# Attention visits, output blocks and loads regrouped around the second and third tile of a linear-attention plus SwiGLU kernel

## Chip, cores, metric

One core of a Trainium2 chip. The metric is device time in microseconds (us) of one execution; lower is better. Before: 229.62 us, median of three runs (228.28 to 232.09).

## The reference, cut

Four sequences of 768 tokens with 8 heads of 64 go through a block-decayed linear attention with blocks of 64 tokens. Its output is `x` (3072 x 512), which goes through a SwiGLU feed-forward network (512 to 1536 to 512).

```python
for b in range(nb):                                  # 12 blocks of 64 tokens
    intra = (q_b @ k_b.T) * Dmask[None]              # decay mask inside the block
    intra = intra @ v_b
    inter = (q_b * lam_pow[None]) @ kv_state         # what earlier blocks left
    out[:, :, sl] = intra + inter
    kv_state = lam_block * kv_state + (k_b * rev_pow).T @ v_b
...
g = x @ w_gate
return (g * sigmoid(g)) * (x @ w_val) @ w_out
```

## The kernel before

The work is cut into 12 **groups**, each two blocks of 128 tokens of one sequence; two groups make a **tile** of 512 tokens, and there are six tiles. For each group the kernel loads k, q and v (512 KB each), casts k and scales q, transposes both (with a DMA from group 3 on, on PE before), and then visits the TensorE (PE) with small attention matmuls. For each tile it runs 12 feed-forward **steps** of eight matmuls of 512 columns (1.73 us; a half step has 256 columns and takes 0.87 us), and then four **output blocks** of 12 matmuls (2.59 us each), each followed by a write of 256 KB.

Attention work is hung between the steps by hand. The order in which it is written is the order on each engine, and PE does it all in that order. (The other engines stand under the profile's names: DVE is VectorE, ACT is ScalarE, POOL is GpSimd, SP is SyncE, which here only issues DMAs; PEld is PE's loading of weights.) While PE does feed-forward work for one tile, the attention of the next tile's groups is slipped in between.

```python
def load_group(g, parts="kqv"):
    for src, what in ((k, "kraw"), (q, "qraw"), (v, "v")):
        if what[0] in parts:
            load_fp32(g, nc.sync, src, what)      # the SP queue

def dma_transpose(g):
    t = st[("qk", g)]
    tt = qkt_pool.tile([128, 2, 2, HP, 128], BF16, name="qkt", tag="qkt")
    nc.sync.dma_start(out=..., in_=..., transpose=True)   # the SP queue too
    st[("qkt", g)] = tt

def cast_scaled(g, eng=nc.vector):
    t = qk_pool.tile([128, 2, 2, H * D], BF16, name="qk", tag="qk")
    st[("qk", g)] = t
    nc.scalar.copy(out=t[:, 0]..., in_=st[("kraw", g)]...)             # ACT casts k
    eng.tensor_tensor(out=t[:, 1]..., in0=st[("qraw", g)]..., in1=qfac(g), op=ALU.mult)  # DVE scales q
    dma_transpose(g)
# ...
def core_a(g):                    # inter: q against the state
    st[("op", g)] = [bank() for _ in range(2)]
    inter(g, True)
    guard(g)                      # a one-column ACT copy that orders inter before intra
def core_b(g, ...):               # intra: masked scores against v
    run_later(len(later))         # the masks (DVE)
    intra(g, False)
    evac(g, fns)                  # ACT copies the result to xt, the input of the tile's steps
def ahead(g):                     # what can be done before core
    upd(g)                        # state update of g: matmuls of k against scaled v
    scores(g)                     # k against q; needs the transpose of g
def attend(g):                    # core of g merged with ahead of g + 1
    run_later(len(later))
    core_a(g)
    if g + 1 < NG:
        upd_mm(g + 1); upd_copy(g + 1)
        scores(g + 1)
        late, later[:] = later[:], []
    core_b(g)
    if g + 1 < NG:
        later[:] = late
        state(g + 1)
# ... the plan: at(step, what) hangs `what` behind that step
s1a = [step(1, fc, 0, 2) for fc in range(FC)]     # second tile in half steps
s1b = [step(1, fc, 2, 4) for fc in range(FC)]
at(s1a[3], cast_scaled, 4)
at(s1a[3], load_group, 5)
for c in range(0, FC, 2):
    at(s1a[3], wo_piece, c, c + 2)                # output weights, 3 MB
# ...
at(s1b[3], cast_scaled, 5)
at(s1b[3], load_group, 6)
at(s1b[6], ahead, 4)
# ...
at(s1b[9], core_a, 4)
at(s1b[10], core_b, 4)
at(s1b[11], ffn_out, 0, 0)
at(s1b[11], ahead, 5)
at(s1b[11], run_later, 3)
at(s1b[11], ffn_out, 0, 1)
at(s1b[11], core_a, 5)
at(s1b[11], ffn_out, 0, 2)
at(s1b[11], core_b, 5)
at(s1b[11], cast_scaled, 6)
at(s1b[11], load_group, 7)
at(s1b[11], v_scale, 6, nc.gpsimd)
at(s1b[11], ffn_out, 0, 3)
outs = [(1, b) for b in range(4)]                 # second tile's outputs: inside the third
for t in range(2, NG // 2):
    ...                                           # steps, cast, load, attend, outputs
```

Loads and transposes leave from one engine's program, SP, in program order: a load written behind a transpose waits until the transposed data has been cast. And groups 0 to 5 load rows of 512 bytes and use a causal mask of double width; groups 6 to 11 load rows of 256 bytes. I call group 6's transpose T6, its loads k6, q6 and v6, and so on.

## Time and profile before

| quantity | before |
|---|---|
| median time | 229.62 us (229.02 with a fourth run) |
| PE busy | 218.5 of 227.1 us |
| largest PE wait after the start-up | 1.21 us |
| T6: issue to landing | 80.16 to 85.84 us |
| T6's data needed on PE | 88.1 us |

The page of the profile: the span, the busy times, and busy tenths in 40 slices of the span for PE and the DMA engines.

```profile
span 227.1 us, 5890 instructions
...
PE 218.5 (96%) x2432; PEld 118.2 (52%) x2444; DVE 90.1 (40%) x154; ACT 106.5 (47%) x209; POOL 88.2 (39%) x129
...
PE   7889999999979999999999999999999999999994
...
PEclk9999999999999999999999999999999999999999
DMA  6999999899997779799877748815101101101122
```

PE is busy almost everywhere, at full clock. Four 512-column matmuls start every 0.863 us, 216 ns each, which agrees with the 215.7 ns that the Trainium skill gives ("TensorE: Matmul & The Clock Gate", section "Wait — 56ns, not 53.3ns?"). So only waits and small matmuls can be saved. The DMA engines are busy too until about two thirds of the span.

The waits of PE (what waited, for what: us in total, times, longest), and the two instructions behind the largest, on the timelines of PE and ACT (start, duration, and in brackets the idle time before it with what ended it).

```profile
PE bank L475 <- ACT guard L446: 1.7, 3, 1.2
PE bank L131 <- DVE warm L125: 1.3, 1, 1.3
```

```profile
65.88 0.64 PE L475 MATMUL bank<-ssb,v_s 64*64 64x128 bf16 x32 [1.21 <-ACT guard L446]
...
88.12 0.46 PE L353 MATMUL bank<-qkt 64*64 64x64 bf16 x32
...
114.81 1.03 PE L517 MATMUL bank<-xt,wg_sb 128*128 128x512 bf16 x4
```

```profile
64.45 1.04 ACT L233 CAST wo_sb<-woraw 128x1024 bf16<-128x1024 f32 x1 [2.24 <-DMA woraw<-in_moe_w_out_dram]
```

The intra of group 4 stood 1.21 us for its guard copy, which stood on ACT behind a cast whose output weights came late. The change aims at this wait. The other two PE lines: group 6's scores start at 88.12 us, and the matmul at 114.81 us begins the fourth tile's steps, from where both kernels have the same order.

The SP timeline (issue time, time that the issue took) around T5 (58.73), T6 (80.16) and T7 (93.18):

```profile
58.73 6.84 SPq L252 DMA_TRANSPOSE qkt<-qk  x1
...
80.16 1.81 SPq L252 DMA_TRANSPOSE qkt<-qk  x1
82.50 2.74 SPq L106 DMA_DIRECT2D kraw<-in_k_dram  x4
85.34 3.14 SPq L106 DMA_DIRECT2D qraw<-in_q_dram  x4
88.53 1.53 SPq L106 DMA_DIRECT2D v<-in_v_dram  x2
93.18 2.00 SPq L252 DMA_TRANSPOSE qkt<-qk  x1
```

All of a group's loads follow the transpose of the group before it, so T6 had only old work ahead of it in the queue. It landed at 85.84 us, 5.7 us after its issue and 2.3 us before PE needed it. T5, behind the output weights, took 10.5 us and still landed 1 us before its use at about 70.3 us.

### The profile page before, as it was taken

How to read it: one execution, taken by the hardware profiler on the slowest of the kernel's cores; microseconds unless marked ns; L12 is line 12 of the kernel's file. 1: busy time of each engine (PE TensorE's matmuls, PEld its weight loads, DVE VectorE, ACT ScalarE, POOL GpSimd, SP SyncE). 2: the span in 40 equal slices, each digit the busy share in tenths (PEclk: the TensorE clock that was granted, in tenths of full speed). 3: DMA queues.
4: the chain of work that ended last, by engine and by line, in shares of the span. 5: the costliest groups of instructions: out<-in, count | busy, mean ns of one | idle time of the engine just before them, and what ended most of it. 6: DMA issues, size and time to landing. Idle time of an engine off the chain costs nothing.

```text
span 227.1 us, 5890 instructions
## 1 busy us (share of the span) xinstructions
PE 218.5 (96%) x2432; PEld 118.2 (52%) x2444; DVE 90.1 (40%) x154; ACT 106.5 (47%) x209; POOL 88.2 (39%) x129
## 2 busy tenths in 40 slices
PE   7889999999979999999999999999999999999994
PEld 3556455878854444454544544544544444444443
DVE  2754357685825214545352362253242123222200
ACT  5868585754652446363454463453433423322221
POOL 6476736642793312978373092092150000000000
PEclk9999999999999999999999999999999999999999
DMA  6999999899997779799877748815101101101122
GB/s 199 345 360 377 367 354 313 210 255 352 300 219 189 206 168 222 177 200 191 217 178 186 185 98 214 214 36 139 49 3 48 46 3 46 46 0 46 49 92 92
DMA packets 88012, 39.70 MB, mean 175 GB/s; under 512 B 57650, under 2 KB 83506, under 8 KB 87986
## 3 DMA queue, kind: packets, MB, share of 16 engines
q1 hardware_dynamic: 83474, 32.64, 55.2%
q10 hardware_dynamic: 4512, 6.69, 8.3%
q8 instruction: 19, 0.31, 0.5%
q14 instruction: 7, 0.06, 0.1%
HBM read 28.31 MB, written 6.29 MB: 152 GB/s over the span
## 4 chain that ended last, share of the span: by engine, by line
PE 84%; DMA 6%; SPq 5%; issue 1%; DVE 1%; ACT 1%; DVEq 0%; ACTq 0%
PE bank L539 27%; PE bank L517 25%; PE bank L524 24%; DMA woraw<-in_moe_w_out_dram 4%; DMA qraw<-in_q_dram 2%; PE bank L475 2%; SPq L99 2%; SPq L228 2%; PE bank L462 2%; PE bank L383 1%; PE bank L353 1%; PE bank L327 1%; PE bank L290 1%; DVE ssb L334 1%; PE bank L168 0%
## 5 line engine op out<-in xcount | busy, mean ns | idle before, releaser
L527 DVE TENSOR_TENSOR h<-sil,bank 128x512 bf16<-128x512 bf16 (+1 forms) x87 | 51.4, 595 | 110.7 <-PE bank L524 94.5
L517 PE MATMUL bank<-xt,wg_sb 128*128 128x512 bf16 (+1 forms) x348 | 76.7, 343 | 0.0
L524 PE MATMUL bank<-xt,wv_sb 128*128 128x512 bf16 (+1 forms) x348 | 76.5, 342 | 0.0
L521 ACT ACTIVATE sil<-bank 128x512 bf16<-128x512 f32 (+1 forms) x87 | 45.8, 528 | 43.4 <-PE bank L517 40.4
L539 PE MATMUL bank<-wo_sb,h 128*128 128x512 bf16 (+1 forms) x288 | 64.2, 370 | 0.7 <-issue 0.2
L524 PEld LDWEIGHTS <-wv_sb 128*128 128x128 bf16 x348 | 34.0, 98 | 28.3
L517 PEld LDWEIGHTS <-wg_sb 128*128 128x128 bf16 x348 | 32.2, 98 | 27.4 <-DVE xt L487 0.5
L539 PEld LDWEIGHTS <-h 128*128 128x128 bf16 x300 | 29.1, 98 | 32.4
L541 ACT COPY osb<-bank 128x512 f32<-128x512 f32 (+1 forms) x24 | 13.8, 576 | 54.9 <-PE bank L539 52.9
L239 POOL TENSOR_TENSOR v_s<-v,dec 128x1024 bf16<-128x1024 f32 (+1 forms) x14 | 23.2, 1665 | 13.9 <-DMA v<-in_v_dram 9.5
L422 POOL TENSOR_TENSOR kvf<-kvs,ups 128x256 f32<-128x256 f32 x8 | 5.8, 726 | 45.1 <-ACT ups L405 40.1
L334 DVE TENSOR_TENSOR ssb<-bank,causal 128x512 bf16<-128x512 f32 x24 | 15.5, 684 | 3.9 <-PE bank L327 3.8
L487 ACT CAST xt<-bank 128x512 bf16<-128x512 f32 x21 | 12.8, 665 | 3.1 <-PE bank L475 2.3
L422 POOL TENSOR_TENSOR kvf<-kvf,ups 128x256 f32<-128x256 f32 x16 | 13.4, 839 | 0.6
L431 POOL CAST kvn<-kvf 64x256 bf16<-64x256 f32 x24 | 11.6, 483 | 1.5
L405 ACT COPY ups<-bank 128x256 f32<-128x256 f32 (+1 forms) x24 | 9.5, 450 | 2.3 <-PE bank L383 1.4
L259 ACT CAST qk<-kraw 128x1024 bf16<-128x1024 f32 x9 | 9.4, 1043 | 0.0
L261 DVE TENSOR_TENSOR qk<-qraw,qdn 128x1024 bf16<-128x1024 f32 x6 | 7.7, 1286 | 3.7 <-DMA qraw<-in_q_dram 3.7
L475 PE MATMUL bank<-ssb,v_s 64*64 64x128 bf16 (+1 forms) x384 | 7.2, 208 | 2.0 <-ACT guard L446 1.7
L222 POOL CAST wv_sb<-wraw 128x1024 bf16<-128x1024 f32 (+1 forms) x7 | 6.4, 918 | 6.1 <-DMA wraw<-in_moe_w_val_dram 6.0
L358 DVE TENSOR_TENSOR ssb<-bank,causaln 128x512 bf16<-128x512 f32 x12 | 8.3, 688 | 1.2 <-PE bank L353 1.1
L233 POOL CAST wo_sb<-woraw 128x1024 bf16<-128x1024 f32 x5 | 5.7, 1171 | 5.3 <-DMA woraw<-in_moe_w_out_dram 5.3
(62 smaller groups left out, 115.6 us busy)
## 6 DMA issues: line engine op xcount, KB each, us to landing
out_dram<-osb ACTq DMA_DIRECT2D x23, 256.0 KB, 2.5
v<-in_v_dram SPq DMA_DIRECT2D x16, 256.0 KB, 4.2
woraw<-in_moe_w_out_dram SPq DMA_DIRECT2D x6, 512.0 KB, 7.1
kraw<-in_k_dram SPq DMA_DIRECT2D x24, 128.0 KB, 3.2
qraw<-in_q_dram SPq DMA_DIRECT2D x24, 128.0 KB, 3.8
wraw<-in_moe_w_gate_dram SPq DMA_DIRECT2D x5, 512.0 KB, 6.6
wraw<-in_moe_w_val_dram SPq DMA_DIRECT2D x5, 512.0 KB, 7.3
kraw<-in_k_dram SPq DMA_DIRECT2D x4, 512.0 KB, 6.5
```

The lines of the kernel that those rows point to most:

```text
L239: eng.tensor_tensor(out=st[("vs", g)][:, h0:h1], in0=st[("v", g)][:, h0:h1].rearrange("p h (s d) -> p h s d", s=2), in1=vfac(g, h0, h1), o ...
L334: nc.vector.tensor_tensor(out=ssb[:, h2, 2 * c:2 * c + 2].rearrange("p a s n -> p a (s n)"), in0=sp[(c, h2)].rearrange("p (a x) -> p a x", ...
L422: nc.gpsimd.tensor_tensor(out=o, in0=f, in1=u, op=ALU.add)
L431: nc.gpsimd.tensor_copy(out=o[64 - h2 * 64:128 - h2 * 64], in_=f[h2 * 64:h2 * 64 + 64])
L475: nc.tensor.matmul(op[r][h2 * 64:h2 * 64 + 64, cols(g, hp, s)], v_s[ps, 2 * hp + h2, s], ssb[ps, h2, hp * 2 + s] if g >= NAT0 else ssb[ps, ...
L487: fns[r](out=xt[:, g % 2, :, r].rearrange("p h (m s) -> p h s m", s=2) if g < NAT0 else xt[:, g % 2, :, :, r * M:r * M + M], in_=op[r].rea ...
L517: nc.tensor.matmul(gp[:, 0:N], wg_sb[:, mc, fs], xt[:, b0 // 2:b1 // 2, mc].rearrange("p g b n -> p g (b n)"), start=(mc == 0), stop=(mc = ...
L521: nc.scalar.activation(sil[:, 0:N], gp[:, 0:N], AF.Silu)
L524: nc.tensor.matmul(vp[:, 0:N], wv_sb[:, mc, fs], xt[:, b0 // 2:b1 // 2, mc].rearrange("p g b n -> p g (b n)"), start=(mc == 0), stop=(mc = ...
L527: nc.vector.tensor_tensor(out=h_sb[:, fc, b0:b1].rearrange("p b n -> p (b n)"), in0=sil[:, 0:N], in1=vp[:, 0:N], op=ALU.mult)
L539: nc.tensor.matmul(ps, h_sb[:, fc, b], wo_sb[:, fc, c0:c1], start=(fc == 0), stop=(fc == FC - 1))
L541: fn(out=osb[:, c0:c1], in_=ps)
```

## The change

Its intent: load the output weights early so that no cast of them stands in the way of attention, do the first tile's output blocks inside the second tile and the second tile's right at its end, merge the scattered visits for groups 4 and 5 into `attend`, and let loads run further ahead: q and v one group, k two groups ahead of the transposes. The core of the diff:

```diff
@@ cast_scaled
         dma_transpose(g)
+        load_group(g + 1, "qv")
+        load_group(g + 2, "k")
@@ first tile
-    at(s0[5], load_group, 3)
+    for c in range(0, FC, 2):
+        at(s0[5], wo_piece, c, c + 2)
     at(s0[6], w_cast)
-    at(s0[7], load_group, 4, "kq")
+    at(s0[7], load_group, 3)
+    at(s0[7], load_group, 4, "k")
@@ second tile (all old lines of it are removed)
+    at(s1a[1], wo_cast)                    # ... and four more casts
+    at(s1a[8], cast_scaled, 3)
+    at(s1a[8], v_scale, 3, nc.gpsimd)
+    at(s1a[8], ffn_out, 0, 0)              # first tile's outputs
+    at(s1a[8], ffn_out, 0, 1)
+    at(s1a[8], ffn_out, 0, 2)
+    at(s1a[8], ahead, 3)
     at(s1a[8], run_later, 2)
+    at(s1a[8], ffn_out, 0, 3)
+    at(s1a[10], core, 3, SPLIT)
+    at(s1a[11], cast_scaled, 4)
+    at(s1a[11], v_scale, 4, nc.gpsimd)
+    at(s1b[5], ahead, 4)
+    at(s1b[9], cast_scaled, 5)
+    at(s1b[9], v_scale, 5, nc.gpsimd)
+    at(s1b[11], ffn_out, 1, 0)             # second tile's outputs
+    at(s1b[11], attend, 4)
+    at(s1b[11], run_later, 2)
     at(s1b[11], cast_scaled, 6)
     at(s1b[11], v_scale, 6, nc.gpsimd)
+    at(s1b[11], ffn_out, 1, 1)
+    at(s1b[11], ffn_out, 1, 2)
+    at(s1b[11], ffn_out, 1, 3)
+    at(s1b[11], attend, 5)
@@ third tile on
-    outs = [(1, b) for b in range(4)]
+    outs = []
     for t in range(2, NG // 2):
-        sn = [step(t, fc) for fc in range(FC)]
         if t == 2:
-            at(sn[2], ahead, 6)
-        for j, g in ((3 if t == 2 else 0, 2 * t + 3), (7 if t == 2 else 6, 2 * t + 4)):
+            sn = [step(t, fc, 0, 2) for fc in range(2)] + [step(t, fc, 2, 4) for fc in range(2)]
+            sn = sn[2:] + [step(t, fc) for fc in range(2, FC)]
+        else:
+            sn = [step(t, fc) for fc in range(FC)]
+        for j, g in ((0, 2 * t + 3), (6, 2 * t + 4)):
             ...
-                if g + 1 < NG:
-                    at(sn[j], load_group, g + 1)
-            at(sn[6 if t == 2 else 4], attend, 2 * t + 2)
+            at(sn[4], attend, 2 * t + 2)
```

Cut from it: the lines at the end of the first tile (group 3's cast, scaling and group 4's v go from there, one cast of output weights comes), and small edits for a sequence's first block beyond group 5, which never apply here.

More of the change, by code (lines that the diff above doesn't have):

```diff
@@ L244, in load_group @@
     def load_group(g, parts="kqv"):
+        if g >= NG:
+            return
         for src, what in ((k, "kraw"), (q, "qraw"), (v, "v")):
@@ L394, in upd_copy @@
         hd = "p (h d) -> p h d"
-        if i == 0 and 0 in parts:
+        if i == 0 and g >= NAT0:
+            st[("kv", g)] = [None]
+        elif i == 0 and 0 in parts:
             kv = kv_pool.tile([128, HP, D], BF16, name="kvn", tag="kvn1", bufs=2)
@@ L455, in inter @@
         started = set()
-        for hp, s, r, h2 in phase(g, first, (1,) if i == 0 else (0, 1) if first else (1, 0)):
+        for hp, s, r, h2 in phase(g, first, (1,) if i == 0 and g < NAT0 else (0, 1) if first else (1, 0)):
             if g < NAT0 and s:
@@ L459, in inter @@
             n = 2 * s + r if g >= NAT0 else r
+            if kv[n] is None:
+                continue
             row, hq = (1 - h2, HP - 1 - hp) if g >= NAT0 and r else (h2, hp)
@@ L477, in intra @@
                              ssb[ps, h2, hp * 2 + s] if g >= NAT0 else ssb[ps, h2, hp, s],
-                             start=((first or (i == 0 and r == 0)) and (r, h2) not in started),
+                             start=((first or (i == 0 and r == 0 and g < NAT0)) and (r, h2) not in started),
                              stop=(not first), skip_group_check=True)
@@ L684, in _body @@
     at(s0["11a"], core, 2, SPLIT)
-    at(s0["11b"], cast_scaled, 3, nc.gpsimd)
-    at(s0["11b"], v_scale, 3, nc.gpsimd)
     at(s0["11b"], state, 2)
-    at(s0["11b"], load_group, 4, "v")
+    at(s0["11b"], wo_cast)
     s1a = [step(1, fc, 0, 2) for fc in range(FC)]
     s1b = [step(1, fc, 2, 4) for fc in range(FC)]
-    at(s1a[3], cast_scaled, 4)
-    at(s1a[3], load_group, 5)
-    for c in range(0, FC, 2):
-        at(s1a[3], wo_piece, c, c + 2)
-    at(s1a[7], scores, 3, (0,))
-    at(s1a[7], run_later, 2)
@@ L698, in _body @@
-    at(s1a[8], scores, 3, (1,))
-    at(s1a[8], upd_mm, 3)
-    at(s1a[8], run_later, 2)
-    at(s1a[8], upd_copy, 3)
-    at(s1a[9], core_a, 3)
-    at(s1a[10], core_b, 3, SPLIT)
-    at(s1a[10], v_scale, 4, nc.gpsimd)
-    at(s1a[10], state, 3)
-    at(s1b[3], cast_scaled, 5)
-    at(s1b[3], load_group, 6)
-    at(s1b[4], wo_cast)
-    at(s1b[4], wo_cast)
-    at(s1b[6], ahead, 4)
-    at(s1b[6], run_later, 2)
-    at(s1b[6], wo_cast)
-    at(s1b[6], wo_cast)
-    at(s1b[6], v_scale, 5, nc.gpsimd)
@@ L715, in _body @@
-    at(s1b[8], wo_cast, ACTC)
-    at(s1b[8], wo_cast)
-    at(s1b[9], core_a, 4)
-    at(s1b[10], core_b, 4)
-    at(s1b[11], ffn_out, 0, 0)
-    at(s1b[11], ahead, 5)
-    at(s1b[11], run_later, 3)
-    at(s1b[11], ffn_out, 0, 1)
-    at(s1b[11], core_a, 5)
-    at(s1b[11], ffn_out, 0, 2)
-    at(s1b[11], core_b, 5)
+    at(s1a[1], wo_cast)
+    at(s1a[3], wo_cast, ACTC)
+    at(s1a[4], wo_cast)
+    at(s1a[5], wo_cast, ACTC)
+    at(s1a[6], wo_cast)
+    at(s1a[8], cast_scaled, 3)
+    at(s1a[8], v_scale, 3, nc.gpsimd)
@@ L726, in _body @@
+    at(s1a[8], ffn_out, 0, 0)
+    at(s1a[8], ffn_out, 0, 1)
+    at(s1a[8], ffn_out, 0, 2)
+    at(s1a[8], ahead, 3)
+    at(s1a[8], run_later, 2)
+    at(s1a[8], ffn_out, 0, 3)
[8 more added lines that the diff above has]
+    at(s1b[11], run_later, 2)
     at(s1b[11], cast_scaled, 6)
-    at(s1b[11], load_group, 7)
@@ L728, in _body @@
     at(s1b[11], v_scale, 6, nc.gpsimd)
-    at(s1b[11], ffn_out, 0, 3)
-    outs = [(1, b) for b in range(4)]
+    at(s1b[11], ffn_out, 1, 1)
[3 more added lines that the diff above has]
+    outs = []
     for t in range(2, NG // 2):
-        sn = [step(t, fc) for fc in range(FC)]
         if t == 2:
-            at(sn[2], ahead, 6)
-        for j, g in ((3 if t == 2 else 0, 2 * t + 3), (7 if t == 2 else 6, 2 * t + 4)):
+            sn = [step(t, fc, 0, 2) for fc in range(2)] + [step(t, fc, 2, 4) for fc in range(2)]
[3 more added lines that the diff above has]
+        for j, g in ((0, 2 * t + 3), (6, 2 * t + 4)):
```

## The prediction

> **What bounds the kernel now.** TensorE does. The page has it busy 218.5 of 227.1 us and the chain that ended last is 84% PE. The timeline shows one feed-forward step of four 512-column matmuls starting every 0.863 us, 216 ns per matmul; "TensorE: Matmul & The Clock Gate" of the Trainium skill (section "Wait — 56ns, not 53.3ns?") gives 215.7 ns as the warm back-to-back spacing, so this part is at its floor. 576 gate and value matmuls and 288 output matmuls at 216 ns are 186.6 us (an estimate from the trace). The rest is about 15 us of start-up, 3 us of tail, and some 20 us of small attention matmuls. From 16 us on, the waits view and the timeline leave under 2 us of real PE idling. The one large wait is 1.21 us at 64.7 us: group 4's second half waits for its guard copy on ACT, which had stood 2.24 us waiting for a late output-weight transfer.
>
> **What the change does.**
> - Output weights (3 MB) go ahead of group 3. At the 1.45 us per 512 KB seen there they land at about 36 to 44 us instead of 57 to 66, so the 1.21 us wait goes, and first-tile outputs fit into the second tile.
> - Groups 4 and 5: seven attention visits (0.92, 0.70, 0.73, 0.92, 0.70, 0.90, 0.76 us in the timeline, about 5.6) become three (about 0.92, 2.1, 1.9). Saves about 0.7 us.
> - Group 3: four visits (2.3 us) become two, but its core now runs unbroken and waits for its own guard, as group 2's does (0.25 us). No gain.
> - Two more split steps: 4 matmuls of 256 columns take 0.4365 us, twice that against 0.863, so +0.02 us.
> - Edits for a first block beyond group 5 never apply here. Matmuls and bytes are otherwise the same.
>
> **What it may add.** Each group's DMA transpose took 3.6 to 5.7 us from issue to landing, issued about 1.9 us after the step that casts. Moved so, group 4's transpose has six half steps (5.2 us) before its scores, group 5's two half steps, one output block and an inter pass (about 5.3 us), and in the now output-free third tile groups 7 and 8 have about 7 us. Each natural-layout group also loads 1.5 MB in about 7.3 us in the same queue, ahead of the next transpose. I expect PE waits at the scores of group 4 (0.3 us), group 5 (0.8), groups 6 and 7 (0.3 each): about 1.7 us. All on the critical path, PE being in order.
>
> **Sum.** -1.2 - 0.2 - 0.7 + 1.7 + small: about -0.5 us. Predicted 228.9 us, range 226.8 to 231.5. Faster by over 2%: 3%; within 2%: 92%; slower: 5%.
>
> **What would show it.** ACT's wait on the output-weight transfer and the 1.21 us PE wait gone; no PE wait before the first output matmul (near 48 us); PE waits at the scores line for groups 4 and 5, released by the transposes; PE busy time and matmul counts unchanged; from the fourth tile on, an identical timeline, shifted by under 1.5 us.
>
> **What would make it wrong.** Transposes queued behind loads for longer, like the 10.5 us one at 58.7 us (then slower by several us), or landing just in time everywhere (then about 2 us faster).  GpSimd (state 6.6 us plus value scaling 1.7 us per group) could be late for group 7. The before times themselves spread 1.7%.

## More of the kernel before

PSUM is a ring of eight banks.

From T5's use to T6's PE had 17.8 us of work.

Busy time of each engine in 10 us windows (columns: window, length, PE, PEld, DVE, ACT, POOL with instruction counts, granted clock, DMA share, GB/s):

```profile
60.00:70.00 10.00, 8.74 (x127) 6.14 (x116) 4.40 (x10) 4.66 (x11) 8.12 (x10) 1.00 0.95 216
...
80.00:90.00 10.00, 10.00 (x108) 4.72 (x107) 2.70 (x4) 4.58 (x9) 1.07 (x3) 1.00 0.87 206
90.00:100.00 10.00, 9.95 (x167) 5.13 (x167) 5.18 (x7) 4.65 (x10) 8.14 (x12) 1.00 0.94 191
```

## The result

The changed kernel takes 237.63 us (median of four runs, 237.19 to 238.80), against 229.02 us (four runs, 228.28 to 232.09). The ratio is 1.0395, with a 95% interval of 1.0333 to 1.0457: slower. Here and below, a ratio is the mean time of one kernel's fast runs over that of the other's fast runs of the same rounds, so it isn't quite the ratio of the medians quoted.

The page after, with the same rows:

```profile
span 235.8 us, 5937 instructions
...
PE 220.4 (93%) x2449; PEld 121.7 (52%) x2460; DVE 92.7 (39%) x157; ACT 108.0 (46%) x212; POOL 85.0 (36%) x127
...
PE   7989999999999795499999999999999999999994
...
PEclk9999999999999999599999999999999999999999
DMA  6999999939758699959896765914011101101122
```

A slice is 5.9 us. PE has a hole in slices 16 and 17, about 88 to 100 us, the second of them at a low mean clock. The DMA row has holes ahead of it, slice 9 (47 to 53 us) and slice 12 (65 to 71 us), where it was full before. The waits of PE and its timeline:

```profile
PE bank L357 <- DMA qkt<-qk: 5.9, 1, 5.9
PE bank L131 <- DVE warm L125: 1.3, 1, 1.3
PE bank L547 <- ACT xt L495: 0.8, 1, 0.8
PE bank L331 <- DMA qkt<-qk: 0.8, 1, 0.8
PE bank L483 <- ACT guard L452: 0.8, 3, 0.3
```

```profile
80.86 0.64 PE L331 MATMUL bank<-qkt 64*64 64x128 bf16 x32 [0.80 <-DMA qkt<-qk]
81.33 0.62 PE L483 MATMUL bank<-ssb,v_s 64*64 64x128 bf16 x32
82.79 7.93 PE L547 MATMUL bank<-wo_sb,h 128*128 128x512 bf16 x35 [0.84 <-ACT xt L495]
...
97.45 0.64 PE L357 MATMUL bank<-qkt 64*64 64x64 bf16 x32 [5.91 <-DMA qkt<-qk]
97.91 1.04 PE L483 MATMUL bank<-ssb,v_s 64*64 64x128 bf16 x32
98.88 1.04 PE L525 MATMUL bank<-xt,wg_sb 128*128 128x256 bf16 x4
...
123.49 1.03 PE L525 MATMUL bank<-xt,wg_sb 128*128 128x512 bf16 x4
```

The old 1.21 us wait has gone. The scores of group 6 (97.45) now stand 5.91 us for T6. Group 5's scores stand 0.80 us for T5, and the output blocks behind them 0.84 us, because the merged visit of a causal group uses all eight banks and the next bank had not been evacuated. Behind the long wait the PE clock is at half: four matmuls of 256 columns, 0.60 us at full clock in this view, are 1.04 us. (A few matmul records are missing from the traces: three output blocks have 36 matmuls, the view found 35.) The trace's clock record says half clock from 94.05 to 100.87 us. The fourth tile's mark comes at 123.49 us, 8.68 us later than before; all of the 8.7 us by which the spans differ is lost by then.

The SP timeline after, around T4 (66.27), T5 (76.94) and T6 (88.15), and the DVE instruction that T6 waited for:

```profile
66.27 1.64 SPq L254 DMA_TRANSPOSE qkt<-qk  x1
...
69.40 3.60 SPq L106 DMA_DIRECT2D kraw<-in_k_dram  x4
76.94 1.66 SPq L254 DMA_TRANSPOSE qkt<-qk  x1
79.12 2.78 SPq L106 DMA_DIRECT2D qraw<-in_q_dram  x4
81.95 2.97 SPq L106 DMA_DIRECT2D v<-in_v_dram  x2
84.97 3.00 SPq L106 DMA_DIRECT2D kraw<-in_k_dram  x4
88.15 3.18 SPq L254 DMA_TRANSPOSE qkt<-qk  x1
```

```profile
86.05 1.23 DVE L263 TENSOR_TENSOR qk<-qraw,qdn 128x1024 bf16<-128x1024 f32 x1 [2.84 <-DMA qraw<-in_q_dram]
```

Read it backward from the wait. T6 landed at 97.41 us. It had been issued at 88.15, late because DVE's scaling of q6 began only at 86.05, having idled 2.84 us for q6, which was issued behind T5 at 79.12. And it took 9.3 us from issue to landing: k7, issued just ahead of it at 84.97, landed at 91.15, and output blocks were written at the same time (issued at 86.20, 88.79 and 91.38, landed at 89.6, 95.9 and 97.8). SP's own waits show how much longer it stood at transposes for DVE's scaling of q (us in total, times, longest), first before and then after:

```profile
SPq L252 <- DVE qk L261: 25.5, 8, 7.2
```

```profile
SPq L254 <- DVE qk L263: 34.7, 8, 10.4
```

While SP stands at a transpose, nothing is issued behind it. The windows after:

```profile
63.00:67.00 4.00, 4.00 (x63) 3.43 (x56) 3.07 (x6) 2.87 (x6) 0.24 (x1) 1.00 0.06 19
...
75.00:78.00 3.00, 2.95 (x22) 2.02 (x21) 2.42 (x4) 1.15 (x3) 0.70 (x1) 1.00 0.04 9
...
60.00:70.00 10.00, 9.75 (x150) 7.98 (x148) 5.73 (x12) 5.55 (x13) 2.61 (x3) 1.00 0.60 171
...
80.00:90.00 10.00, 8.30 (x103) 4.33 (x99) 3.71 (x5) 4.16 (x8) 4.73 (x6) 1.00 0.82 206
90.00:100.00 10.00, 4.09 (x122) 2.96 (x121) 0.69 (x1) 2.75 (x6) 5.83 (x11) 0.70 1.04 200
```

From 63 to 67 us the DMA engines were at 0.06 of their time (19 GB/s): SP stood at T4. From 75 to 78 us they were at 0.04: SP stood at T5, whose q5 had landed at 72.1 us while its scaling on DVE began only at 75.35, where the plan has it. (A third hole, 0.07 from 103 to 106 us, lies before T7, behind the long wait.) From 90 to 100 us they were full (1.04 in this view) and PE was at 4.09 of 10 us.

An account of the 8.7 us from these two profiles: +5.91 (T6), +0.80 (T5), +0.84 (banks), +0.5 (two short waits for a mask's bank), about +1.5 for half clock (a visible 0.15 us in the scores, 0.4 in the intra, 0.97 in the half steps behind), +0.6 because this profile's start-up was later (the first inter of group 1 at 17.21 against 16.62 us; the start-ups of all profiles here spread over 1.3 us), less 1.4 us of waits that the kernel before had around group 4. That is 8.7 us with nothing left for a gain elsewhere; the half-clock term is an estimate, so this says only that the merged visits gained well under 1 us.

### The profile page after: what moved, and what is told of

Its sections match the earlier page's. It is cut to its first block, busy times and chain, and to the rows that moved or that the text cites. A ratio compares the mean times of both kernels' runs of the same rounds, so it can differ in the third digit from the quotient of the medians.

```text
span 235.8 us, 5937 instructions
## 1 busy us (share of the span) xinstructions
PE 220.4 (93%) x2449; PEld 121.7 (52%) x2460; DVE 92.7 (39%) x157; ACT 108.0 (46%) x212; POOL 85.0 (36%) x127
## 4 chain that ended last, share of the span: by engine, by line
PE 84%; DMA 7%; SPq 3%; DVE 3%; issue 1%; ACT 1%; DVEq 0%
PE bank L525 26%; PE bank L532 26%; PE bank L547 22%; DMA qkt<-qk 4%; DMA kraw<-in_k_dram 3%; SPq L106 2%; PE bank L483 2%; PE bank L294 1%; PE bank L470 1%; PE bank L387 1%; PE bank L331 1%; DVE ssb L338 1%; PE bank L357 1%; PE bank L168 1%; SPq L254 1%
## 5 line engine op out<-in xcount | busy, mean ns | idle before, releaser
L532 PE MATMUL bank<-xt,wv_sb 128*128 128x512 bf16 (+1 forms) x356 | 77.3, 340 | 0.3 <-DVE ssb L338 0.3
L525 PE MATMUL bank<-xt,wg_sb 128*128 128x512 bf16 (+1 forms) x356 | 77.6, 341 | 0.0
L532 PEld LDWEIGHTS <-wv_sb 128*128 128x128 bf16 x356 | 35.1, 98 | 28.2 <-issue 0.5
L525 PEld LDWEIGHTS <-wg_sb 128*128 128x128 bf16 x356 | 33.7, 99 | 27.1 <-DVE xt L495 0.4
L547 PEld LDWEIGHTS <-h 128*128 128x128 bf16 x300 | 29.2, 98 | 33.2 <-issue 0.8
L437 POOL CAST kvn<-kvf 64x256 bf16<-64x256 f32 x24 | 12.6, 526 | 1.5
L428 POOL TENSOR_TENSOR kvf<-kvf,ups 128x256 f32<-128x256 f32 x16 | 12.4, 778 | 0.6
L357 PE MATMUL bank<-qkt 64*64 64x64 bf16 x192 | 3.3, 204 | 5.9 <-DMA qkt<-qk 5.9
L483 PE MATMUL bank<-ssb,v_s 64*64 64x128 bf16 (+1 forms) x384 | 7.7, 215 | 1.0 <-ACT guard L452 0.8
```

Of the source, the lines that this page charges most:

```text
L428: nc.gpsimd.tensor_tensor(out=o, in0=f, in1=u, op=ALU.add)
L437: nc.gpsimd.tensor_copy(out=o[64 - h2 * 64:128 - h2 * 64], in_=f[h2 * 64:h2 * 64 + 64])
L483: nc.tensor.matmul(op[r][h2 * 64:h2 * 64 + 64, cols(g, hp, s)], v_s[ps, 2 * hp + h2, s], ssb[ps, h2, hp * 2 + s] if g >= NAT0 else ssb[ps, ...
L525: nc.tensor.matmul(gp[:, 0:N], wg_sb[:, mc, fs], xt[:, b0 // 2:b1 // 2, mc].rearrange("p g b n -> p g (b n)"), start=(mc == 0), stop=(mc = ...
L532: nc.tensor.matmul(vp[:, 0:N], wv_sb[:, mc, fs], xt[:, b0 // 2:b1 // 2, mc].rearrange("p g b n -> p g (b n)"), start=(mc == 0), stop=(mc = ...
L547: nc.tensor.matmul(ps, h_sb[:, fc, b], wo_sb[:, fc, c0:c1], start=(fc == 0), stop=(fc == FC - 1))
```

## The experiments

The theory: T6 lands late because of the **DMA queue**. Three things make it so: q6 stands behind T5, k7 stands ahead of T6, and second-tile outputs are written beside it. All three come from the same move: with no output blocks left in the third tile, PE needs groups 6, 7 and 8 some 10 to 12 us apart, and the queue needs about that for one group.

Rivals: one **single cause** among the three, with the others harmless; the **spacing** on PE alone, so that visiting group 5 later mends it; the **merged visit**, which asks for T6 before group 5's intra and so exposes a wait that scattered visits would hide; and, for the gain that didn't come, that the early output weights were worth **nothing**.

Edits are against the changed kernel except in the two whose label begins with p, which edit the kernel before. Each was timed in three rounds (one in five) against the kernel before on the same chip.

### Only k7's place

```diff
         dma_transpose(g)
+        if g == 6:
+            load_group(7, "k")
         load_group(g + 1, "qv")
-        load_group(g + 2, "k")
+        if g != 5:
+            load_group(g + 2, "k")
```

> The changed kernel, with group 7's k load moved from ahead of group 6's transpose to just behind it in the queue. In the changed kernel that transpose was issued at 88.2 us, its queue emptied of k loads at 91.2 us, it landed at 97.4 us, and TensorE waited 5.9 us for it. Theory QUEUE (it stands behind the k load): landing 3 us sooner, the wait near 2.5 to 3 us, ratio to before near 1.02. Theory INPUT (group 6's q comes late, so cast and issue are late): issue and landing hardly move, wait over 5 us, ratio near 1.04. Theory WRITE (output transfers running at the same time slow it): the transpose still takes over 6 us from the moment it is at the head of the queue, wait 3 to 6 us.

Ratio of fast runs 1.0204 (1.0128 to 1.0280), four runs of 232.86 to 238.07 us. Two of them, the profiled one included, are slow runs with a clock of 0.983 to 0.984; the ratio uses the other two. I read from the profile only when things landed. T6 went from 9.3 us to 4.8 us (88.42 to 93.24), as the queue theory says, and its wait from 5.91 to 1.24 us. But group 7 paid:

```profile
93.28 0.45 PE L360 MATMUL bank<-qkt 64*64 64x64 bf16 x32 [1.24 <-DMA qkt<-qk]
...
105.85 0.64 PE L390 MATMUL bank<-v_s,qk 64*64 64x64 bf16 x32 [2.33 <-POOL v_s L239]
...
107.56 0.64 PE L360 MATMUL bank<-qkt 64*64 64x64 bf16 x32 [1.06 <-DMA qkt<-qk]
```

Group 7's v came 2.33 us late and T7 1.06 us late, in a stretch that then ran at half clock (105.65 to 112.48 us). k7's place is a real part of the cause, but a moved wait is not a removed one.

### q6 ahead of T5

```diff
-        load_group(g + 1, "qv")
-        load_group(g + 2, "k")
+        load_group(g + 1, "v" if g == 5 else "qv")
+        load_group(g + 2, "kq" if g == 4 else "k")
```

> The changed kernel, with group 6's q load moved from behind group 5's transpose to ahead of it, behind group 6's k. Theory INPUT: the cast of group 6 no longer waits 2.8 us for q, its transpose is issued about 3 us sooner relative to the visit of group 4, and the 5.9 us wait shrinks to 2 to 3 us. Theory QUEUE: less stands between the two transposes, so the same wait shrinks to below 2 us, but group 5's transpose now stands behind the q load and the wait at group 5's scores grows from 0.8 to about 3 us. Ratio to before near 1.02 by both; WRITE alone would leave the wait at 3 us or more.

231.98 us, ratio 1.0122 (1.0061 to 1.0183). T6 was issued at 85.62 instead of 88.15 and landed at 89.83, ahead of its need; nothing waited for it or for T7. For T5, about 3 us of waiting had been expected; 1.25 us came, and of this kind that is all that remains:

```profile
81.82 0.64 PE L331 MATMUL bank<-qkt 64*64 64x128 bf16 x32 [1.25 <-DMA qkt<-qk]
```

This uses the hole at 63 to 67 us no better, but it puts 512 KB into the next one, the stretch in which SP stood at T5. Two edited lines brought back more than half of the loss. The clock stayed at 1.0 in this profile.

### Writes of the second tile held back

The last three output blocks are computed where they were, but written only after the visit of group 5 (a fourth output buffer; six would not fit the SBUF).

```diff
+            def send(c0=c0, c1=c1, eng=eng):
                 eng.dma_start(...)
+            if t == 1 and b > 0: held.append(send)
+            else: send()
@@
     at(s1b[11], attend, 5)
+    at(s1b[11], send_held)
```

> The changed kernel, with the last three output transfers of the second tile held back until the visit of group 5 is over (one more buffer for them). Theory WRITE: group 6's transpose takes 3.6 to 4 us from the head of the queue instead of 6.3 and lands near 95 us, so the wait falls from 5.9 to about 3.5 us, ratio near 1.025. Theory QUEUE and theory INPUT: no change in the landing beyond 0.5 us, ratio near 1.04.

234.66 us, ratio 1.0238 (1.0195 to 1.0281). T6 took 4.3 us (88.69 to 92.95), although k7 was still ahead of it and landed at 91.0; no theory had it land before 95. So taking away either k7 or the writes brings it to 4 to 5 us; in these runs only both together make it 9. In this run the waits for T5 (1.17 us) and the banks (0.84 us) fell close together and one clock window (83.03 to 86.44 us) ran at half clock: the three output blocks took 9.6 us instead of 7.9, which by itself hid a part of T6. T7 then came 1.02 us late.

### Group 5 visited later

```diff
-    at(s1b[11], attend, 5)
@@
-            sn = [step(t, fc, 0, 2) for fc in range(2)] + [step(t, fc, 2, 4) for fc in range(2)]
-            sn = sn[2:] + [step(t, fc) for fc in range(2, FC)]
+            sn = [step(t, fc, 0, 2) for fc in range(4)]
+            at(sn[3], attend, 5)
+            sn = [step(t, fc, 2, 4) for fc in range(4)] + [step(t, fc) for fc in range(4, FC)]
@@
-            at(sn[4], attend, 2 * t + 2)
+            at(sn[5 if t == 2 else 4], attend, 2 * t + 2)
```

> The changed kernel, with the visit of group 5 put behind four half steps of the third tile on group 4 alone (3.5 us of matmuls), and as many half steps on group 5 behind it. All loads and the transpose as they were. If the whole loss is that TensorE comes to the visit before the transpose has landed: the wait shrinks by 3.5 us to about 2.4 us, and the slow clock after it (granted 0.70 between 90 and 100 us) goes as well, so the time falls by 4.5 to 5 us, ratio near 1.018. If something else holds the time (the queue of loads overall), the wait moves to the next visits, groups 6 and 7, and the ratio stays over 1.03.

234.32 us, ratio 1.0228 (1.0180 to 1.0275). T6 took 6.5 us and nobody waited for it: spacing does hide it. The time went elsewhere: 1.50 us for T5, 0.84 for banks, a half-clock window at 82.79 to 86.20, then 0.78 us for a mask's bank and 1.69 us at the evacuation of group 5, which four half steps no longer cover. A later visit is a trade, not a cure.

### All loads one group ahead

```diff
-        load_group(g + 1, "qv")
-        load_group(g + 2, "k")
+        load_group(g + 1)
@@
-    at(s0[7], load_group, 4, "k")
```

> The changed kernel with one part undone: each group's k, q and v are loaded together behind the transpose of the group before, as in the kernel before, instead of k two groups ahead. Nothing but group 6's v then stands between group 6's q and its transpose, but k and q of group 6 both come behind transpose 5. If the far-ahead k load is what made the loss: the transpose of group 6 lands by 92 us and the 5.9 us wait is under 1 us. If the bytes that the queue must move between the two transposes are what matters, with whatever order: issue near 90 us, landing 94 to 95 us, a wait of 3 us, ratio to before near 1.02.

234.51 us, ratio 1.0233 (1.0187 to 1.0280), all four runs at a clock of 0.993. T6 took 3.7 us (89.00 to 92.73), the shortest of all, and PE waited 1.17 us for it, 0.47 for v, 0.56 for T4, 0.37 for T5, 0.36 for T7 and 0.84 for banks. With nothing ahead of the transposes they are quick, and every one is late by a little: both k and q now stand behind the transpose before. The result lies between the two that were expected. A half-clock window followed (93.78 to 97.19).

### Group 5's visit taken apart

```diff
-    at(s1b[11], attend, 5)
+    at(s1b[11], core_a, 5)
+    at(s1b[11], core_b, 5)
@@
+            if t == 2:
+                at(sn[1], ahead, 6)
-            at(sn[4], attend, 2 * t + 2)
+            at(sn[6 if t == 2 else 4], attend, 2 * t + 2)
```

> The changed kernel with one part undone: the visit of group 5 no longer holds group 6's update and scores; these come as a visit of their own three and a half microseconds of matmuls later, in the third tile, as in the kernel before. Loads and transposes as in the changed kernel. If the merge is what brought the need for transpose 6 ahead of its landing: the 5.9 us wait falls to 2 us or less, the half clock behind it goes, and the time falls by 5 to 7 us, ratio 1.005 to 1.015. If the queue alone were at fault whoever asks, the wait would move and the ratio stay over 1.025.

236.89 us, ratio 1.0342 (1.0283 to 1.0400): nearly as slow as the change, so the merged visit as the cause falls. PE's wait for T6 shrank to 0.16 us, although it took 8.2 us. In its place came 0.73 us for a guard, 1.28 us behind DVE (which waited 3.69 us for q7), and 2.32 us for the scaled v of group 8 at 118.58: GpSimd had waited 11.63 us for v7, and the work behind it kept it from scaling v8 before 116.61. The same lateness came out at another consumer.

### A repair of all that was seen

q6 early as above; two output blocks ahead of the visit of group 4; two banks skipped behind it; the visit of group 5 between the third tile's half steps.

```diff
-        load_group(g + 1, "qv")
-        load_group(g + 2, "k")
+        load_group(g + 1, "v" if g == 5 else "qv")
+        load_group(g + 2, "kq" if g == 4 else "k")
@@
     at(s1b[11], ffn_out, 1, 0)
+    at(s1b[11], ffn_out, 1, 1)
     at(s1b[11], attend, 4)
+    at(s1b[11], skip_banks)                 # ring[0] += 2
@@
-    at(s1b[11], ffn_out, 1, 1)
@@
-    at(s1b[11], attend, 5)
@@
+            sn = [step(t, fc, 0, 2) for fc in range(4)]
+            at(sn[1], attend, 5)
+            sn = [step(t, fc, 2, 4) for fc in range(4)] + [step(t, fc) for fc in range(4, FC)]
```

> A repair: group 6's q loaded ahead of transpose 5, a second output block ahead of the visit of group 4 (so that transpose 5, later by 2 us, is there in time), the visit of group 5 behind two half steps of the third tile with two more behind it, and the first bank after the visit of group 4 not one that its evacuation still holds. All waits on transposes and the 0.84 us wait on the evacuation should be gone, and with them the half clock: about 226.5 to 228 us in the profile, ratio 0.99 to 1.0. If I have missed a limit (GpSimd's state, transposes 7 and 8), waits of 1 us or more show at groups 6 to 8 and the ratio stays over 1.0.

230.26 us (229.93 to 230.54), ratio 1.0049 (1.0012 to 1.0085), clock 1.0. That is short of the 0.99 to 1.0 that was expected. No wait for a DMA transpose over 0.1 us is left. T6 landed at 90.78, T7 at 102.89 and T8 at 113.86 us: 12.1 and 11.0 us apart, with the DMA engines at 0.90 of their time from T5's landing to T8's. One wait of 1.28 us for a mask stands (and 0.30 us for the scaled v of group 8):

```profile
91.11 0.60 PE L532 MATMUL bank<-xt,wv_sb 128*128 128x256 bf16 x4 [1.28 <-DVE ssb L338]
```

So nearly the whole loss can be mended, and what comes out is no better than the kernel before.

### The same, with that mask run earlier (five rounds)

```diff
     at(s1b[11], cast_scaled, 6)
+    at(s1b[11], run_later, 1)
```

> The repair, with the fourth mask of group 5 emitted right behind group 6's cast instead of behind the next half step, where its bank held TensorE for 1.28 us. That wait gone: 1 to 1.3 us less than the repair, ratio to before 0.998 to 1.002. If the mask's bank was only covering for transpose 6, a wait of about 1 us shows at group 6's scores and the ratio stays at 1.004 to 1.006.

230.49 us (six runs, 229.44 to 231.08), ratio 1.0070 (1.0027 to 1.0113): nothing gained. The mask's wait went, and T7 and T8 came late by 0.80 and 0.50 us instead (T6, where the expectation looked, did not). The mask's wait had only covered the transposes'; in this stretch the supply of transposed groups sets the pace.

### The early output weights' gain, by itself, in the kernel before

```diff
-    at(s1b[8], wo_cast, ACTC)
@@
     at(s1b[10], core_b, 4)
+    at(s1b[10], wo_cast, ACTC)
```

> The kernel before with one move: the output-weight cast on ACT that made the 1.21 us wait stands behind the second half of group 4's visit instead of ahead of it. That wait gone and no other in its place: 1.2 us less, ratio 0.995. This is what the early output weights could win at most. If the ratio stays at 1.000, the wait was slack of something else.

228.96 us, ratio 0.9998 (0.9953 to 1.0043). The 1.21 us wait is gone, and one of 0.42 us behind a cast on GpSimd stands in its place. From the scores of group 3 to those of group 6 the profile is 0.68 us shorter than that of the kernel before (47.73 to 87.67 against 47.50 to 88.12 us), but the interval of the times is 1 us wide to either side. The wait that the change was to remove was worth nothing that the timing can show.

### Group 6's scores without T6 (wrong result)

```diff
-        tt = st[("qkt", g)]
+        tt = st[("qkt", 5 if g == 6 else g)]     # in scores_n
```

> The changed kernel, wrong on purpose: group 6's scores read group 5's transposed tile, which is there long before, so TensorE need not wait for transpose 6 at that visit; every transfer, cast and matmul is as in the changed kernel, and transpose 6 itself is first needed 17 us later. If the loss is that one wait and the half clock behind it: 5.9 us and 1.5 to 1.7 us go, ratio to before 1.005 to 1.012. If the queue of loads is over-full as a whole, TensorE meets the next transposes, 7 and 8, earlier and waits there instead: ratio over 1.02.

The result is wrong, as meant (relative error 6.86). Ratio of fast runs 1.0290 (1.0222 to 1.0358), 236.15 us. The profiled run is a slow one. With the wait for T6 taken away altogether, PE reached group 7 earlier and stood there:

```profile
105.39 0.64 PE L387 MATMUL bank<-v_s,qk 64*64 64x64 bf16 x32 [2.76 <-POOL v_s L239]
...
107.56 0.64 PE L357 MATMUL bank<-qkt 64*64 64x64 bf16 x32 [1.52 <-DMA qkt<-qk]
```

Only about a quarter of the loss came back (1.0395 to 1.0290; the two are from different rounds, and their intervals overlap). This is the strongest evidence against a single cause: the 5.91 us wait is where a queue that is behind shows itself first, not what it costs.

### k two groups ahead in the kernel before

```diff
     at(s1b[3], load_group, 6)
+    at(s1b[3], load_group, 7, "k")
@@
-    at(s1b[11], load_group, 7)
+    at(s1b[11], load_group, 7, "qv")
+    at(s1b[11], load_group, 8, "k")
@@
-                    at(sn[j], load_group, g + 1)
+                    at(sn[j], load_group, g + 1, "qv")
+                if g + 2 < NG:
+                    at(sn[j], load_group, g + 2, "k")
```

> The kernel before, with the k loads from group 7 on put one group further ahead, as in the change; nothing else. Transpose 7 and the later ones then stand behind a k load that they did not stand behind. In the kernel before each has about 10 us between its cast and its scores, so if the far load costs only where slack is short: transposes land up to 2 us later, no new wait on TensorE, ratio 0.997 to 1.003. If the far load costs by itself: waits at the scores of groups 7 to 11, ratio over 1.01.

228.72 us, ratio 1.0011 (0.9954 to 1.0067). T6 79.88 to 84.97, T7 92.89 to 98.34, T8 104.20 to 109.49 us, and no new wait. Running k two groups ahead does no harm where PE gives the queue 42 us for what the change gives it 33 (from T5's use to T8's).

### Fewer bytes (wrong result)

```diff
+        if g in (6, 7) and "v" in parts:
+            st[("v", g)] = st[("v", g - 4)]      # v of groups 6 and 7 isn't loaded
+            parts = parts.replace("v", "")
```

> The changed kernel, wrong on purpose: the v of groups 6 and 7 is not loaded (512 KB each less; the tiles of groups 2 and 3 stand in), so that the queue has a third less to move between transposes 5, 6 and 7. Order, casts and matmuls as in the changed kernel. If the third tile asks for groups faster than the queue brings them (11 to 13 us a group): transposes 6 and 7 land 3 us or more sooner, nothing waits at group 7, the wait at group 6 falls below 2.5 us, ratio to before 1.005 to 1.015. If it is the chain of cast, issue and transpose of each group and not the bytes: transpose 6 is issued at 88 us still, the waits stay over 4 us in all, ratio over 1.025.

The result is wrong, as meant (relative error 0.63). 231.95 us, ratio 1.0120 (1.0052 to 1.0188). T6 took 5.0 us and PE waited 1.50 us for it instead of 5.91; nothing waited for T7; T5 was 1.02 us late, much as in the changed kernel. A wait of 1.37 us for the scaled v of group 2, at 38.3 us, is in this profile too; it lies ahead of the edited loads. Taking 1 MB from the queue, and its four issues from SP, does as much as issuing q6 earlier. What is left of the waits goes with q6, which is issued as late as before (T6 issued at 89.14).

## Why the prediction was wrong

The prediction was 228.9 us, at most 231.5, with 5% for "slower by over 2%". The result is 237.6 us.

**The step that failed** is "I expect PE waits at the scores of group 4 (0.3 us), group 5 (0.8), groups 6 and 7 (0.3 each): about 1.7 us." Measured: group 4 none, group 5 0.80, group 6 **5.91**, group 7 none. The mechanism was named, and group 5's size is right; the term for group 6 was too small by 5.6 us. Under it lies the prediction's "3.6 to 5.7 us from issue to landing": T6 took 9.3 us (88.15 to 97.41), and it was issued late. The issue was late because q6 stood behind T5 in SP's program, shown by q6 early (T6 issued at 85.62, no wait). The landing took 9.3 us because k7 was ahead and writes were beside it, shown by taking away each (4.8 and 4.3 us).

**Under that step lies a wrong balance.** I counted that "in the now output-free third tile groups 7 and 8 have about 7 us" and that a group loads 1.5 MB "in about 7.3 us", and never set the whole queue against the whole PE work of the stretch. Moving the second tile's output blocks forward takes about 10 us of PE work without loads out of the third tile. Before, PE used T5 to T8 within 41.9 us (17.8, 10.6, 13.5). With q6 early, where nothing waited for T6, T7 or T8 and the clock was full, it used them within 33.2 us (10.5, of which 0.84 for banks, 11.0 and 11.8): most of the slack went between T5 and T6. From T5's landing to T8's it took 33.0 us with q6 early and 33.2 with the repair, with the DMA engines at 0.93 and 0.90 of their time. So the queue has next to nothing to spare there, while in the changed kernel it idled from 63 to 67 and from 75 to 78 us because loads stood behind T4 and T5. That the supply was behind in the whole stretch, and not at one wait, is shown by the free scores (1.029, waits at group 7), by fewer bytes (1.012) and by the same bytes earlier (1.012). How much of it is too many bytes, and how much loads that are issued too late, these runs do not part; casting group 5 earlier, so that SP would not stand at T5, is the obvious run that was not made.

**Terms that I left out.** Half clock: about 1.5 us in this profile. Banks: 0.84 us, in every variant but the repaired ones. Neither is in the prediction.

**"-1.2 - 0.2" for the wait at group 4.** The wait and the ACT wait went, and no PE wait stood before the first output matmul (48.87 us; predicted near 48). But the cast moved alone in the kernel before gave 0.9998, and 0.68 us in the profile: there the time wasn't all to be had. Whether the term was mis-sized in the change itself isn't shown.

**"-0.7" for merging groups 4 and 5.** Measured as the predicted figures were (from where the steps or output blocks ahead would have been done, at their own pace, to the start of those behind), the three visits, without waits, are 0.99, 2.07 and 2.42 us, the last with about 0.5 us of half clock; predicted 0.92, 2.1, 1.9. These are right. Group 3's visits took 2.43 us against 2.25 before, where I said "no gain", so about 0.5 us is left.

**"from the fourth tile on, an identical timeline, shifted by under 1.5 us".** Identical, yes; shifted by 8.7 us.

**What would make it wrong** named it: "Transposes queued behind loads for longer ... (then slower by several us)". I gave it 5% because the 10.5 us T5 of before had cost nothing, and didn't ask how long PE could do without it (11.6 us from its issue to its use, then).

The Trainium skill would have pointed here. "DMA: Bandwidth & Descriptors", section "Queues, rings and completion order", has descriptors of one ring consumed in order and each DMA engine going round between the rings by packets. The trace agrees with both as far as landings can tell: T6 landed behind k7 of its own queue (91.15 us), and the writes of the other queue landed while T6 was pending.

**Open.** T6 took 9.3, 8.2, 7.9 and 6.5 us in the four runs (the change, the visit taken apart, the free scores, the later visit) in which blocks were being written and k7 landed 2.4 to 3.9 us after T6's issue. In these four the issue itself took 3.1 to 3.9 us. In the other variants of the changed kernel, where either was missing, T6 took 3.7 to 5.0 us (3.7 to 4.8 behind no k7, 4.3 with the writes held, 4.2 and 5.0 where k7 landed within 1.8 us of the issue). Why two things that each cost about a microsecond cost four or five together was observed, not explained. A part of it is one straggler: of the sixteen completions that the trace has for T6 in the changed kernel, fifteen came between 95.69 and 96.02 us and the last at 97.41. T5 before shows the same (67.68 and 69.19 us).

**Whether to keep any of it.** No version beat the kernel before. The best, the repair, is 0.5% slower; how much the change could have gained at most wasn't measured.

## What to carry to other kernels

Before moving compute that needs no loads (here output blocks) out of a stretch, set for that stretch the time between two uses of a loaded group against the time in which the queue can deliver one, whole cycles and not single latencies; the moved work was the queue's slack. When a wait stands out, free its consumer (even with a wrong result): if the waiting turns up again elsewhere, the supply is short; here fewer bytes or an earlier issue helped. A wait that the chain names is worth what comes back when it alone is removed, which here was too little for the timing to show, and that test costs one run.

## What the Trainium skill lacked or had wrong

- "TensorE: Matmul & The Clock Gate", section "HAM oscillation — how this bites in real kernels", gives as the abstract rule no idle gaps over about 3.4 us; for shorter idles that come close together the page has no length. Here, with writes held, waits of 1.17 and 0.84 us (between 79.6 and 82.7 us) were followed by a window at half clock (83.03 to 86.44 us). In the changed kernel 0.80 and 0.84 us were not, nor 1.25 and 0.84 us with q6 early, so their sum alone does not decide. The half-clock stretches inside the kernels are 3.41 or 6.83 us long, which agrees with the window of 3413 ns and the two-valued clock of the section "What's actually happening".
- "DMA: Bandwidth & Descriptors", section "Latency and other measured facts", gives an effective rate of 261 GB/s for a DMA transpose whose middle dimension is not contiguous, and no latency beside other traffic. In the changed kernel and its variants this SBUF-to-SBUF transpose of 512 KB (T6) took 3.7 us from issue to landing with no load ahead of it, 4.3 us with a load ahead, 3.7 to 4.8 us with writes beside it, and up to 9.3 us with both; in the kernel before T6 took 5.7 us with a write beside it, and T5 10.5 us behind the output weights. The issue itself, 1.6 to 2.0 us, grew to 3.18 us (T6) and to 6.84 us (T5 before).
- The same page, section "Rules for kernel authors", says that a transpose next to ordinary DMAs needs nothing. That is about corruption, and no run here contradicts it (all runs that were meant to be right were); it has no word on time, where T6 took from 3.7 to 9.3 us by what was in flight with it.
- No page that I read spells out that a load written behind a transpose in one engine's program waits for the transpose's input: SP stood 34.7 us in all at transposes for DVE's scaling of q (25.5 before), and the DMA engines were at 0.06 from 63 to 67 us.
